# Moving the upper half of the attention weights from GpSimd to ScalarE

## The chip, the cores and the metric

One core of one Trainium2 chip runs the whole program. The metric is the device time of one launch in microseconds (us). The kernel before takes 861.48 us, the median of three runs (859.91 to 862.36).

## What is computed

Three layers in a row: an attention with a mask by hash buckets, a dense feed-forward with a gated activation, and a mixture of 8 experts of which each token takes two. Cut to what matters here:

```python
# attention: batch 2, heads 8, sequence 768, head size 64
mask = q_bucket[:, :, :, None] == k_bucket[:, :, None, :]
scores = np.where(mask, scale * q @ k.T, -1e9)
scores = scores - scores.max(-1, keepdims=True)
attn = np.exp(scores)
attn = attn / (attn.sum(-1, keepdims=True) + 1e-9)
x = attn @ v                       # becomes 1536 tokens of 512
# feed-forward, 512 -> 2048 -> 512
h = x @ w_in
x = (h / (1 + np.exp(-1.702 * h))) @ w_out
# experts: a noisy gate picks 2 of 8; 512 -> 1024 -> 512, relu between, weighted sum
```

## The kernel before

TensorE multiplies float16. To keep float32's accuracy, each factor is split into a high float16 part and a low one (the rest), and a product is three passes: high by high, high by low, low by high.

The attention runs in 96 units g = 0 to 95; a unit is one head and 128 queries, and 16 units make one chunk of 256 tokens. For a unit:

- `qk` (L252): TensorE makes the scores of 128 queries by 768 keys in PSUM (tile `s`, two buffers); the mask is part of the product.
- `rowmax` (L261, L262): VectorE takes the row's maximum and scales it (`mx`).
- `expo` (L271): ScalarE makes the exponentials into `e32` (two buffers), with the row's sum. From unit 28 on (`NG` = 28) VectorE makes the reciprocal of the sum from it at once (L275, L276); before, the sum is used later, behind the product.
- `e_hi` (L308), from unit 16 on: the **upper half**, `er[:, 0]`, float16, is `e32` times the reciprocal (or times 1.0 for units 16 to 27). GpSimd makes it. `er` has two buffers.
- `e_lo` (L319; L317 for units 16 to 27): the lower half, `er[:, 1]`, on VectorE (three of the units 16 to 27 on GpSimd). Behind it SyncE's queue issues a transposing DMA of both halves (L323) into `et`.
- `pv` (L364): TensorE multiplies the transposed weights by `v`.

So `e_hi` of unit g needs the exponential, the reciprocal, and that the transposing DMA of unit g-2 has read its buffer of `er`; and `expo` of unit g+2 needs that `e_lo` of unit g has read its buffer of `e32`.

The first 16 units take another way (float32, transposed on TensorE) and have no `e_hi`. Beside the attention run: the preparation of q and k (L142 to L209) and of v (L228 to L235), the splitting of the feed-forward's weights (L424 to L442), the feed-forward of the chunk before (L456 on TensorE, L474 on ScalarE, L486 on VectorE, L500 on ScalarE, L501 on GpSimd; then L467), and the routing (L586 to L679). After the attention come the last chunk's feed-forward, its routing, and the experts (L735 to L830), which TensorE fills.

Each engine works through its own queue in order. For the attention these orders aren't written out by hand: up to step 100 of the loop a planner orders each engine's instructions by the program's order and by its own estimate of when each one is ready. From step 100 on (the attention's last unit is 95) the order is that of the program.

`PARAM` holds the choices, among them the engine of `e_hi` by unit, `HI`, which is `'PPPP'[g%4]` in the line that counts (L56). `e_hi` itself has both ways already:

```python
        if PARAM["HI"](g) == "P":
            nc.gpsimd.tensor_scalar(er[:, 0], st[g]["e"], r, 1.0, op0=OP.mult, op1=OP.mult)
        else:
            nc.scalar.activation(er[:, 0], st[g]["e"], AF.Copy, scale=r)
```

Of the kernel before, what the change touches and what calls it, by code (L numbers as in the profile page):

```python
# [23 lines left out]
CAP = 432  # L24
REG = 256
# [29 lines left out]
PARAM = dict(GM=16, HE=lambda nm, b: 'D', OE=lambda nm, b: 'D', SC=lambda nm, b: 'D', WB=0, XO=lambda b: 'D', NG=16, WS=lambda i: 'P', TS=lambda g: True, XL=lambda g: 'D', GW=2, E0=7, T0=12, T1=16, EL=8, WX=3, PV={(1,2,3):4}, PVD=5, ST={}, VA={}, RA={}, O0=48, OS=2, IS=2, FU=16, VF=2, EC=lambda g: 'AA', QX=8, QS=3, EA=1, S1=(8,8,8,9,9,9,11,13), QE=8, XG=2, XB=2, PC=2, OH=3, BK=3, R0=18, R1=0, LK=8, WL=1, NW=3, LE=lambda nc: nc.scalar, I0=24, LQ=8, LV=0, W=[(g, 1) for g in range(-6, 30)], KA={(0,0,0):-8,(0,0,1):-6,(0,1,0):-4,(0,1,1):-2}, QA={(0,0,0):-7,(0,0,1):-3}, HI=lambda g: 'P', LO=lambda g: False)  # L55
PARAM.update(KA={(0, 0, 0): -15, (0, 0, 1): -6, (0, 1, 0): -5, (0, 1, 1): -4, (0, 2, 0): -1, (0, 2, 1): 1, (0, 3, 0): 4, (0, 3, 1): 5, (1, 0, 0): 37, (1, 0, 1): 39, (1, 1, 0): 44, (1, 1, 1): 46, (1, 2, 0): 42, (1, 2, 1): 51, (1, 3, 0): 47, (1, 3, 1): 51}, QA={(0, 0, 0): -15, (0, 0, 1): -3, (0, 0, 2): 1, (0, 0, 3): 3, (0, 1, 0): 8, (0, 1, 1): 9, (0, 1, 2): 17, (0, 1, 3): 21, (0, 2, 0): 24, (0, 2, 1): 28, (0, 2, 2): 30, (0, 2, 3): 33, (1, 0, 0): 37, (1, 0, 1): 41, (1, 0, 2): 47, (1, 0, 3): 52, (1, 1, 0): 57, (1, 1, 1): 56, (1, 1, 2): 60, (1, 1, 3): 69, (1, 2, 0): 72, (1, 2, 1): 69, (1, 2, 2): 80, (1, 2, 3): 84}, VA={(0, 0, 0): -1, (0, 0, 1): -3, (0, 1, 0): -1, (0, 1, 1): -1, (0, 2, 0): 0, (0, 2, 1): 0, (0, 3, 0): -1, (0, 3, 1): -2, (1, 0, 0): -1, (1, 0, 1): -1, (1, 1, 0): 2, (1, 1, 1): -4, (1, 2, 0): -3, (1, 2, 1): -3, (1, 3, 0): 2, (1, 3, 1): -2}, PV={(0, 0, 0): 4, (0, 0, 1): 5, (0, 0, 2): 6, (0, 0, 3): 5, (0, 1, 0): 6, (0, 1, 1): 4, (0, 1, 2): 4, (0, 1, 3): 5, (0, 2, 0): 5, (0, 2, 1): 5, (0, 2, 2): 5, (0, 2, 3): 6, (1, 0, 0): 4, (1, 0, 1): 5, (1, 0, 2): 4, (1, 0, 3): 5, (1, 1, 0): 5, (1, 1, 1): 5, (1, 1, 2): 5, (1, 1, 3): 6, (1, 2, 0): 6, (1, 2, 1): 4, (1, 2, 2): 4, (1, 2, 3): 4}, RA={0: 18, 1: 18, 2: 19, 3: 24, 4: 18}, W=[(g,1) for g in [-6, -4, -3, -1, 0, 0, 1, 1, 2, 4, 4, 7, 8, 8, 9, 10, 11, 12, 13, 14, 15, 16, 16, 17, 18, 20, 20, 22, 22, 23, 23, 24]], EC=lambda g:'AA', LE=lambda nc:nc.sync, HI=lambda g:'PPPP'[g%4], LO=lambda g:[0, 0, 0, 1, 0, 0, 0, 1][g%8]==1, S1=[8, 8, 8, 8, 8, 11, 13, 22], ST={0: 4, 1: 4, 2: 5, 3: 4, 4: 5, 5: 3}, NG=28, WS=lambda i:'PAAA'[i%4], HE=lambda nm,b:'DPDD'[2*(nm=='k')+b], OE=lambda nm,b:'DTDD'[2*(nm=='k')+b], SC=lambda nm,b:'DADD'[2*(nm=='k')+b], R1=2, I0=16, IS=2, O0=56, OS=1, GM=100, BK=3, OH=3, QX=8, QS=2, QE=7, VF=0, T0=12, T1=17, EL=10, WX=5, WL=2, PC=2, GW=2, E0=8, WB=2)  # L56


@with_exitstack
def fused(ctx: ExitStack, tc: tile.TileContext, q, k, v, proj, w_in, w_out, w_gate, w_noise, noise,  # L60
          w1, w2, out, dbg=None):
    nc = tc.nc
# [25 lines left out]
    def proj_parts():  # L88
        p32 = rt.tile([128, NBITS], F32, name="p32", tag="zc", bufs=1)
        nc.sync.dma_start(p32[:64], proj)  # L90
        nc.sync.dma_start(p32[64:], proj)
        # proj in three parts; the first ones of x and proj lie on grids, so that their products add exactly
        p3 = rt.tile([128, 3, NBITS], F16, name="p3", tag="z", bufs=1)
        nc.vector.tensor_scalar(p3[:, 0], p32, GP, GP, op0=OP.add, op1=OP.subtract)
        nc.vector.tensor_tensor(p32, p32, p3[:, 0], op=OP.subtract)
        nc.vector.tensor_copy(p3[:, 1], p32)
        nc.vector.tensor_tensor(p32, p32, p3[:, 1], op=OP.subtract)
        for nm, a0 in (("q", 0), ("k", 64)):
            w = pr[nm]
            h, l = slice(a0, a0 + 64), slice(64 - a0, 128 - a0)  # L100
            nc.vector.tensor_scalar(w[h, 0], p3[h, 0], SH, 0.0, op0=OP.mult, op1=OP.add)
            nc.vector.tensor_scalar(w[h, 1], p3[h, 1], -SH, 0.0, op0=OP.mult, op1=OP.add)
            nc.vector.tensor_scalar(w[h, 2], p32[h], -SH, 0.0, op0=OP.mult, op1=OP.add)
            nc.vector.memset(w[l, 0], 0.0)
            nc.vector.tensor_scalar(w[l, 1:3], p3[l, 0:2], -1.0 / SH, 0.0, op0=OP.mult, op1=OP.add)
# [3 lines left out]

# [1 line left out]
    raw, rows, kts, qts, vts, bks = {}, {}, {}, {}, {}, {}  # L111
    FL = "p h c d -> p (h c) d"

    # q: both heads of a pair, one chunk (u = pair, chunk); k and v: one head (u = pair, head)
    def load(nm, b, u):
# [12 lines left out]
    def stack_hi(nm, b, u):  # L128
        x = raw[nm, b, u]
        nh, n = (2, CT) if nm == "q" else (1, NT)  # L130
        if nm == "q":
            sa = att.tile([128, nh, n, 128], F16, name="qsa", bufs=1)
            sb = att.tile([128, nh, n, 128], F16, name="qsb", bufs=2)
        else:
            # in the place of what the feed-forward needs later, or no longer
            ks = moe.tile([128, 2, n, 128], F16, name="ks", tag="wraw" if b else "gt", bufs=PARAM["NW"] if b else 4)
            sa, sb = ks[:, 0:1], ks[:, 1:2]
# [75 lines left out]

    # the first units take float32 products, which need fewer passes of the other engines
    def v_load32(cc, hp):
# [20 lines left out]

# [1 line left out]
    st, ets, xts, pos, sms = {}, {}, {}, {}, {}  # L238
# [156 lines left out]

# [1 line left out]
    wi = [wts.tile([128, HP, FF], F16, name=f"wi{i}", tag="w") for i in range(2)]  # L397
# [105 lines left out]

# [1 line left out]
    before = consts.tile([128, 128], F16)  # L505
# [60 lines left out]
    def route(ci):  # L566
# [15 lines left out]
        zn = z[:, :, E:]  # L582
        # log(1 + exp(zn)) = max(zn, 0) + y with y = log(1 + t), t = exp(-|zn|), by Newton's steps
        w = rt.tile([128, 6, CT, E], F32, name="rw", bufs=1)
# [45 lines left out]
        yield  # L630
        # the row's last columns: token, first expert, both weights
        me = mst[ci, "xr"][:, :, 2 * DM:].bitcast(F32)
# [52 lines left out]

    # the first experts' first REG slots are read before the last chunk is routed: its tokens come behind them
    def reserve():
# [25 lines left out]

# [1 line left out]
    ew, eblk, xg, met, hts, yst = {}, {}, {}, {}, {}, {}  # L715
# [21 lines left out]

    # the slots of an expert: in one part, or in two
    def parts(e):
        return ((0, REG), (REG, CAP)) if e < EA else ((0, CAP),)  # L740

    def e_load(e, p):
# [12 lines left out]
        if nr:  # L755
            # the last 64 slots, twice; those that the tile before holds too go to spare rows
            nc.vector.tensor_copy(mf[:, nf], blank2)
            for h in range(2):
                nc.sync.dma_start(mf[h * 64 + 64 - nr:h * 64 + 64, nf], slots[r0 + 128 * nf:r0 + n, 2 * DM:])
# [73 lines left out]

# [1 line left out]
    todo, first, early = {}, {}, {}  # L835
# [22 lines left out]

    # the steps of several chains by turns
    def by_turns(chains):  # L860
# [49 lines left out]
    steps = {}  # L910
# [76 lines left out]
    for n, (e, p) in enumerate(gs):  # L987
        begin[e, p] = len(seq)
        c0, c1 = parts(e)[p]
        l1s = [("1", e, p, f) for f in range(FE // 128)]  # L990
        l2s = [("2", e, p, t) for t in range(c0 // 128, -(-c1 // 128))]
        # the next one's first product comes before this one's second
        if n and (p == 0 or n > EA):
            seq.insert(hold, l1s.pop(0))
        seq += l1s
        hold = len(seq)
        seq += l2s
# [33 lines left out]

# [1 line left out]
    most = nc.values_load(cnt_i[0:1, E:E + 1], min_val=0, max_val=N)  # L1033
    with tc.If(most > CAP):
        with tc.tile_pool(name="ov", bufs=1) as ov:
# [13 lines left out]
            with tc.For_i(0, E, 1) as e:  # L1049
# [5 lines left out]
                with tc.If(here > CAP):  # L1055
# [12 lines left out]
                    with tc.For_i(0, (OV + 127) // 128, 1) as k_:  # L1068
                        with tc.If(here > k_ * 128 + CAP):
                            # the row of this lane, or the last one of the expert  # L1070
                            nc.vector.tensor_tensor(val, blk, lane, op=OP.add)
# [10 lines left out]
                            me = row[:, 2 * DM:].bitcast(F32)  # L1082
                            # its token, or a spare row of the output
                            nc.vector.tensor_copy(tmp, me[:, 0:1].bitcast(I32))
                            nc.vector.scalar_tensor_tensor(tmp, tmp, float(N), lane, op0=OP.subtract, op1=OP.subtract)
                            nc.vector.tensor_tensor(tmp, tmp, ok, op=OP.mult)
                            nc.vector.scalar_tensor_tensor(ints[:, 1:2], tmp, float(N), lane, op0=OP.add, op1=OP.add)
                            # its weight
                            sc = 1.0 / (SX2 * SW1 * SW2)
# [51 lines left out]
```

## Time and profile before

| | |
|---|---|
| median of three runs | 861.48 us |
| profiled execution, first to last instruction | 857.1 us |
| TensorE busy | 734.4 us (86%) |
| VectorE busy | 563.0 us (66%) |
| ScalarE busy | 380.9 us (44%) |
| GpSimd busy | 358.5 us (42%) |
| units with an `e_hi` | 80, from 97.1 to 482.0 us |

The profile shows one execution. PE is TensorE's matrix products, PEld its weight loads, DVE VectorE, ACT ScalarE, POOL GpSimd, SP SyncE; a small q behind a name is the engine's sequencer. The chain of work that ended last is followed back from the last instruction, at each step to what released it. "Idle before" is how long an engine stood just before an instruction, and the name behind it is what ended that.

### The profile page before, as it was taken

To read this page: it belongs to the slowest core of one execution; us is meant where nothing else is said; L and a number is where in the kernel's file an instruction comes from. 1 tells how busy PE (TensorE), PEld (TensorE's weight loads), DVE (VectorE), ACT (ScalarE), POOL (GpSimd) and SP (SyncE) were. 2 spreads that over 40 slices of the span, in tenths; PEclk is the share of its full clock that TensorE was granted. 3 is DMA by queue.
4 is the path that set the end of the run, shared out by engine and by line. 5 is a ranking of instruction groups with operands and counts; after the bars stand their busy time and mean duration, and the time that the engine had idled before them with its cause. 6 is when DMAs were issued, how large, how long until landed. Compare 5 with 4: busy or idle time off the path is not lost.

```text
span 857.1 us, 14808 instructions
## 1 busy us (share of the span) xinstructions
PE 734.4 (86%) x5398; PEld 449.4 (52%) x5399; DVE 563.0 (66%) x1327; ACT 380.9 (44%) x779; POOL 358.5 (42%) x352
## 2 busy tenths in 40 slices
PE   1577687868888789888988999779999999999994
PEld 1354465436644565466567575546554555545542
DVE  8998799998997699579778626444533535335210
ACT  3687656545644464254335235243433534335210
POOL 6355478775846466456535333141021121211212
PEclk9878798999999989999999999989999999999997
DMA  8999999998989978986787533766875847757212
GB/s 202 224 246 234 208 212 209 220 196 157 182 150 200 170 150 184 234 159 112 131 150 118 106 141 112 185 184 158 222 158 171 205 110 202 160 163 167 37 13 39
DMA packets 285453, 141.03 MB, mean 165 GB/s; under 512 B 231552, under 2 KB 264384, under 8 KB 285376
## 3 DMA queue, kind: packets, MB, share of 16 engines
q1 hardware_dynamic: 278848, 126.37, 68.2%
q0 software_dynamic: 6528, 13.68, 8.7%
q8 instruction: 43, 0.70, 0.3%
q14 instruction: 34, 0.28, 0.1%
HBM read 61.49 MB, written 24.25 MB: 100 GB/s over the span
## 4 chain that ended last, share of the span: by engine, by line
PE 38%; DVE 29%; DMA 16%; issue 6%; POOL 5%; ACT 3%; SPq 1%; POOLq 0%; DVEq 0%; ACTq 0%
PE ph L792 16%; PE py L814 12%; DMA et<-er 6%; DVE er L319 6%; DVE mx L261 5%; PE h L456 4%; DMA slots<-xr,si 2%; PE py L818 2%; PE px L467 2%; POOL er L308 2%; POOL slots L679 2%; DMA qt<-qsb 2%; DMA out_dram<-yo,ti 2%; DVE wf L424 2%; ACT e L271 2%
## 5 line engine op out<-in xcount | busy, mean ns | idle before, releaser
L456 PE MATMUL h<-xt,wi 128*128 128x256 f16 x1152 | 145.6, 281 | 12.2 <-DVE th L486 8.2
L792 PE MATMUL ph<-xg,ew 128*128 128x432 f16 (+2 forms) x864 | 146.7, 334 | 9.5 <-DMA xg<-slots 9.5
L830 POOL DMA_INDIRECT out_dram<-yo,ti x32 | 52.7, 1648 | 231.3 <-ACT yo L828 168.8
L467 PE MATMUL px<-wo,gt 128*128 128x512 f16 x576 | 133.2, 382 | 5.9 <-ACT wo L441 3.3
L736 DVE SCALAR_TENSOR_TENSOR ew<-w,ew 128x1024 f16<-128x1024 f32 x64 | 77.9, 1226 | 89.3 <-ACT ew L735 89.3
L456 PEld LDWEIGHTS <-wi 128*128 128x128 f16 x1152 | 113.9, 101 | 36.4 <-issue 13.7
L271 ACT ACTIVATE e<-s,mx 128x768 f32<-128x768 f32 x96 | 86.0, 897 | 93.9 <-DVE mx L262 63.4
L814 PE MATMUL py<-ew,ht 128*128 128x512 f16 x576 | 125.8, 379 | 0.0
L792 PEld LDWEIGHTS <-ew 128*128 128x128 f16 x864 | 85.2, 101 | 69.1 <-issue 6.2
L252 PE MATMUL s<-kt,qt 128*128 128x512 f16 (+1 forms) x384 | 88.6, 354 | 26.6 <-ACT e L271 20.5
L308 POOL TENSOR_SCALAR er<-e,mx 128x768 f16<-128x768 f32 x68 | 69.1, 1017 | 88.7 <-DMA et<-er 29.5
L319 DVE SCALAR_TENSOR_TENSOR er<-e,mx,er 128x768 f16<-128x768 f32 x68 | 77.8, 1144 | 25.6 <-POOL er L308 25.5
L467 PEld LDWEIGHTS <-gt 128*128 128x128 f16 x576 | 55.3, 98 | 70.6 <-issue 9.2
L261 DVE TENSOR_REDUCE mx<-s 128x1 f32<-128x768 f32 x96 | 90.2, 944 | 2.1 <-PE s L252 2.0
L814 PEld LDWEIGHTS <-ht 128*128 128x128 f16 x576 | 56.4, 98 | 67.2
L803 DVE SCALAR_TENSOR_TENSOR ht<-ph,ht 128x432 f16<-128x432 f32 (+2 forms) x72 | 40.0, 556 | 57.0 <-ACT ht L802 56.1
L501 POOL TENSOR_TENSOR gt<-th,gt 128x512 f16<-128x512 f32 x48 | 61.0, 1270 | 34.2 <-ACT gt L500 33.2
L802 ACT ACTIVATE ht<-ph 128x432 f16<-128x432 f32 (+2 forms) x72 | 35.2, 490 | 84.3 <-PE ph L792 84.3
L735 ACT ACTIVATE ew<-w 128x1024 f16<-128x1024 f32 x64 | 66.3, 1047 | 2.5 <-DMA w<-in_moe_w_dram 2.5
L252 PEld LDWEIGHTS <-qt 128*128 128x128 f16 x384 | 37.2, 103 | 56.6 <-issue 31.1
L828 ACT ACTIVATE yo<-py,wv 128x512 f32<-128x512 f32 (+1 forms) x32 | 20.3, 633 | 102.7 <-PE py L814 54.6
L364 PE MATMUL pv<-et,vt 128*64 128x256 f16 x720 | 50.9, 280 | 8.7 <-DMA et<-er 7.3
(192 smaller groups left out, 958.1 us busy)
## 6 DMA issues: line engine op xcount, KB each, us to landing
w<-in_moe_w_dram SPq DMA_DIRECT2D x64, 512.0 KB, 4.2
wraw<-in_moe_w_in_dram SPq DMA_DIRECT2D x16, 512.0 KB, 4.3
wraw<-in_moe_w_out_dram SPq DMA_DIRECT2D x16, 512.0 KB, 5.1
slots<-zeros SPq DMA_DIRECT2D x27, 256.0 KB, 7.2
v<-in_v_dram SPq DMA_DIRECT2D x24, 192.0 KB, 4.1
out_dram<-zeros SPq DMA_DIRECT2D x13, 256.0 KB, 3.2
k<-in_k_dram SPq DMA_DIRECT2D x16, 192.0 KB, 3.0
q<-in_q_dram SPq DMA_DIRECT2D x48, 64.0 KB, 3.7
```

Source lines behind the costliest of these rows:

```text
L252: nc.tensor.matmul(ps[:, n0 * 128:n1 * 128], qt[:, s, h, t, :], kt[:, s, h, n0:n1, :].rearrange("p c t -> p (c t)"), start=(s == 0), stop= ...
L261: nc.vector.reduce_max(mx[:, 0:1], st[g]["ps"][:, :S], axis=AX.X)
L271: nc.scalar.activation(e32, st[g]["ps"][:, :S], AF.Exp, scale=0.125, bias=st[g]["mx"][:, 1:2], accum_out=sms[b, cc, hp][:, 2 * h + t:2 * h ...
L308: nc.gpsimd.tensor_scalar(er[:, 0], st[g]["e"], r, 1.0, op0=OP.mult, op1=OP.mult)
L319: nc.vector.scalar_tensor_tensor(er[:, 1], d["e"], d["mx"][:, 3:4], er[:, 0], op0=OP.mult, op1=OP.subtract)
L456: nc.tensor.matmul(ph[:, a, :], wi[ws][:, d, f0:f0 + 128], xt[:, d, xs, :], start=(d == 0 and ws == 0 and xs == 0), stop=(d == HP - 1 and ...
L467: nc.tensor.matmul(px, gts[ci, f // 2][:, gs, f % 2, t * 128:t * 128 + 128], wo[ws][:, f, :], start=(f == 0 and gs == 0 and ws == 0), stop ...
L501: nc.gpsimd.tensor_tensor(gt[:, 1], th, gt[:, 0], op=OP.subtract)
L735: nc.scalar.activation(hi, x, AF.Copy, scale=SW1 if j == 0 else SW2)
L736: nc.vector.scalar_tensor_tensor(lo, x, SW1 if j == 0 else SW2, hi, op0=OP.mult, op1=OP.subtract)
L792: nc.tensor.matmul(ph[:, :c1 - c0], w[:, ws, d * FE + f * 128:d * FE + f * 128 + 128], xg[e, p][:, xs * HP + d, :], start=(d == 0 and ws = ...
L814: nc.tensor.matmul(py, ht[:, f, hs, t * 128:t * 128 + 128], w[:, ws, f * DM:(f + 1) * DM], start=(i == 0), stop=(i == n - 1))
```

## The change

`HI` gives `A` for each unit: `e_hi` takes the other branch, an activation Copy with the reciprocal (or 1.0) as scale, in ScalarE's queue. All 80 of the GpSimd instructions at L308 become ScalarE instructions at L310. The rest of the diff removes comments. All other choices, buffers and orders in the program's text stay.

```diff
 PARAM.update(
...
-HI=lambda g:'PPPP'[g%4],
+HI=lambda g:'AAAA'[g%4],
...
 )
```

## Rows read from the trace of the kernel before

**Rows 1.** The page: busy time of each engine; the chain's shares by engine and line

```profile
PE 734.4 (86%) x5398; PEld 449.4 (52%) x5399; DVE 563.0 (66%) x1327; ACT 380.9 (44%) x779; POOL 358.5 (42%) x352
PE 38%; DVE 29%; DMA 16%; issue 6%; POOL 5%; ACT 3%; SPq 1%; POOLq 0%; DVEq 0%; ACTq 0%
PE ph L792 16%; PE py L814 12%; DMA et<-er 6%; DVE er L319 6%; DVE mx L261 5%; PE h L456 4%; DMA slots<-xr,si 2%; PE py L818 2%; PE px L467 2%; POOL er L308 2%; POOL slots L679 2%; DMA qt<-qsb 2%; DMA out_dram<-yo,ti 2%; DVE wf L424 2%; ACT e L271 2%
```

**Rows 2.** Windows: stretch, its length, busy time of each engine, clock, DMA share, GB/s

```profile
95.00:300.00 205.00, 166.00 (x1379) 107.14 (x1378) 182.27 (x402) 105.47 (x233) 131.27 (x117) 0.95 1.01 190
300.00:485.00 185.00, 165.69 (x1375) 110.53 (x1375) 149.91 (x403) 81.61 (x194) 100.44 (x93) 0.97 0.79 150
485.00:530.00 45.00, 44.63 (x345) 30.44 (x344) 16.05 (x56) 16.17 (x30) 13.25 (x13) 1.00 0.36 111
530.00:575.00 45.00, 35.27 (x219) 20.61 (x218) 23.29 (x78) 15.12 (x29) 14.50 (x17) 0.95 0.70 185
575.00:857.00 282.00, 269.48 (x1681) 147.09 (x1680) 106.55 (x190) 99.18 (x145) 50.03 (x31) 0.97 0.59 141
```

**Rows 3.** The chain that ended last, whole span, by line

```profile
by line: PE ph L792 16.1%; PE py L814 12.1%; DMA et<-er 6.4%; issue 6.3%; DVE er L319 5.7%; DVE mx L261 4.7%; PE h L456 3.5%; DMA slots<-xr,si 2.4%; PE py L818 2.2%; PE px L467 2.0%; POOL er L308 1.9%; POOL slots L679 1.9%; DMA qt<-qsb 1.8%
```

**Rows 4.** Groups by form: count, busy us, mean ns, idle before and its releasers

```profile
L308 POOL TENSOR_SCALAR er<-e,mx 128x768 f16<-128x768 f32 x68 | 69.1, 1017 | 88.7 <-DMA et<-er 29.5 <-DVE mx L276 19.0 <-DVE mx L275 6.0
L308 POOL TENSOR_SCALAR er<-e 128x768 f16<-128x768 f32 x12 | 12.4, 1029 | 6.6 <-DMA et<-er 5.2 <-PE pv L357 1.2
L319 DVE SCALAR_TENSOR_TENSOR er<-e,mx,er 128x768 f16<-128x768 f32 x68 | 77.8, 1144 | 25.6 <-POOL er L308 25.5
```

**Rows 5.** Timeline around 367 us: start us, us, engine, line; idle before

```profile
367.47 0.88 ACT L271 ACTIVATE e<-s,mx 128x768 f32<-128x768 f32 x1
...
368.35 0.89 ACT L271 ACTIVATE e<-s,mx 128x768 f32<-128x768 f32 x1
...
369.00 0.90 POOL L308 TENSOR_SCALAR er<-e,mx 128x768 f16<-128x768 f32 x1 [1.26 <-DVE mx L276]
...
369.22 0.59 ACT L474 ACTIVATE th<-h 128x512 f32<-128x512 f32 x1
```

**Rows 6.** Groups by form on ScalarE, whole span: copies of other widths, the exponential

```profile
L156 ACT ACTIVATE qsa<-q 128x256 f16<-128x256 f32 x24 | 9.9, 412 | 6.5 <-POOL q L143 4.4 <-issue 1.9
...
L735 ACT ACTIVATE ew<-w 128x1024 f16<-128x1024 f32 x64 | 66.3, 1047 | 2.5 <-DMA w<-in_moe_w_dram 2.5
...
L271 ACT ACTIVATE e<-s,mx 128x768 f32<-128x768 f32 x96 | 86.0, 897 | 93.9 <-DVE mx L262 63.4 <-DVE er L319 14.5 <-DVE mx L276 3.6
```

**Rows 7.** Three lines of VectorE: count, then ns min/median/max of one, first and last start

```profile
L319 DVE SCALAR_TENSOR_TENSOR er<-e,mx,er x68: 992/1018/2531, 172.0 to 483.2; 128x768 f16<-128x768 f32 x68
...
L198 DVE TENSOR_SCALAR qsb<-iota_i,bk x48: 216/232/1215, 238.7 to 454.0; 128x64 f16<-128x64 f16 x48
...
L424 DVE TENSOR_SCALAR wf<-wraw x32: 407/427/1377, 8.0 to 188.5; 128x512 int32<-128x512 int32 x32
```

**Rows 8.** Groups by form on VectorE, 95 to 485 us

```profile
L198 DVE TENSOR_SCALAR qsb<-iota_i,bk 128x64 f16<-128x64 f16 x48 | 15.0, 377 | 0.1
...
L424 DVE TENSOR_SCALAR wf<-wraw 128x512 int32<-128x512 int32 x15 | 11.2, 749 | 2.1 <-DMA wraw<-in_moe_w_out_dram 2.1
```

**Rows 9.** Windows of line L308 alone

```profile
95.00:485.00 390.00, 81.49 (x80) 0.96 0.91 171
```

**Rows 10.** Tile er: how long its transposing DMA takes to land, of 80

```profile
DMA to landing us min/median/max: 3.7/3.9/8.2
```

**Rows 11.** Timeline around 299 us

```profile
298.37 0.91 POOL L308 TENSOR_SCALAR er<-e,mx 128x768 f16<-128x768 f32 x1 [4.56 <-DMA et<-er]
...
299.31 1.02 DVE L319 SCALAR_TENSOR_TENSOR er<-e,mx,er 128x768 f16<-128x768 f32 x1 [3.73 <-POOL er L308]
299.80 1.30 POOL L308 TENSOR_SCALAR er<-e,mx 128x768 f16<-128x768 f32 x1 [0.52 <-DMA et<-er]
...
300.31 0.83 DVE L189 TENSOR_TENSOR pc<-pc,pow 128x36 f32<-128x36 f32 x1
...
300.51 0.90 ACT L271 ACTIVATE e<-s,mx 128x768 f32<-128x768 f32 x1 [5.75 <-DVE mx L262]
```

More of the change, by code (lines that the diff above doesn't have):

```diff
@@ L55 @@
 PARAM = dict(GM=16, HE=lambda nm, b: 'D', OE=lambda nm, b: 'D', SC=lambda nm, b: 'D', WB=0, XO=lambda b: 'D', NG=16, WS=lambda i: 'P', TS=lambda g: True, XL=lambda g: 'D', GW=2, E0=7, T0=12, T1=16, EL=8, WX=3, PV={(1,2,3):4}, PVD=5, ST={}, VA={}, RA={}, O0=48, OS=2, IS=2, FU=16, VF=2, EC=lambda g: 'AA', QX=8, QS=3, EA=1, S1=(8,8,8,9,9,9,11,13), QE=8, XG=2, XB=2, PC=2, OH=3, BK=3, R0=18, R1=0, LK=8, WL=1, NW=3, LE=lambda nc: nc.scalar, I0=24, LQ=8, LV=0, W=[(g, 1) for g in range(-6, 30)], KA={(0,0,0):-8,(0,0,1):-6,(0,1,0):-4,(0,1,1):-2}, QA={(0,0,0):-7,(0,0,1):-3}, HI=lambda g: 'P', LO=lambda g: False)
-PARAM.update(KA={(0, 0, 0): -15, (0, 0, 1): -6, (0, 1, 0): -5, (0, 1, 1): -4, (0, 2, 0): -1, (0, 2, 1): 1, (0, 3, 0): 4, (0, 3, 1): 5, (1, 0, 0): 37, (1, 0, 1): 39, (1, 1, 0): 44, (1, 1, 1): 46, (1, 2, 0): 42, (1, 2, 1): 51, (1, 3, 0): 47, (1, 3, 1): 51}, QA={(0, 0, 0): -15, (0, 0, 1): -3, (0, 0, 2): 1, (0, 0, 3): 3, (0, 1, 0): 8, (0, 1, 1): 9, (0, 1, 2): 17, (0, 1, 3): 21, (0, 2, 0): 24, (0, 2, 1): 28, (0, 2, 2): 30, (0, 2, 3): 33, (1, 0, 0): 37, (1, 0, 1): 41, (1, 0, 2): 47, (1, 0, 3): 52, (1, 1, 0): 57, (1, 1, 1): 56, (1, 1, 2): 60, (1, 1, 3): 69, (1, 2, 0): 72, (1, 2, 1): 69, (1, 2, 2): 80, (1, 2, 3): 84}, VA={(0, 0, 0): -1, (0, 0, 1): -3, (0, 1, 0): -1, (0, 1, 1): -1, (0, 2, 0): 0, (0, 2, 1): 0, (0, 3, 0): -1, (0, 3, 1): -2, (1, 0, 0): -1, (1, 0, 1): -1, (1, 1, 0): 2, (1, 1, 1): -4, (1, 2, 0): -3, (1, 2, 1): -3, (1, 3, 0): 2, (1, 3, 1): -2}, PV={(0, 0, 0): 4, (0, 0, 1): 5, (0, 0, 2): 6, (0, 0, 3): 5, (0, 1, 0): 6, (0, 1, 1): 4, (0, 1, 2): 4, (0, 1, 3): 5, (0, 2, 0): 5, (0, 2, 1): 5, (0, 2, 2): 5, (0, 2, 3): 6, (1, 0, 0): 4, (1, 0, 1): 5, (1, 0, 2): 4, (1, 0, 3): 5, (1, 1, 0): 5, (1, 1, 1): 5, (1, 1, 2): 5, (1, 1, 3): 6, (1, 2, 0): 6, (1, 2, 1): 4, (1, 2, 2): 4, (1, 2, 3): 4}, RA={0: 18, 1: 18, 2: 19, 3: 24, 4: 18}, W=[(g,1) for g in [-6, -4, -3, -1, 0, 0, 1, 1, 2, 4, 4, 7, 8, 8, 9, 10, 11, 12, 13, 14, 15, 16, 16, 17, 18, 20, 20, 22, 22, 23, 23, 24]], EC=lambda g:'AA', LE=lambda nc:nc.sync, HI=lambda g:'PPPP'[g%4], LO=lambda g:[0, 0, 0, 1, 0, 0, 0, 1][g%8]==1, S1=[8, 8, 8, 8, 8, 11, 13, 22], ST={0: 4, 1: 4, 2: 5, 3: 4, 4: 5, 5: 3}, NG=28, WS=lambda i:'PAAA'[i%4], HE=lambda nm,b:'DPDD'[2*(nm=='k')+b], OE=lambda nm,b:'DTDD'[2*(nm=='k')+b], SC=lambda nm,b:'DADD'[2*(nm=='k')+b], R1=2, I0=16, IS=2, O0=56, OS=1, GM=100, BK=3, OH=3, QX=8, QS=2, QE=7, VF=0, T0=12, T1=17, EL=10, WX=5, WL=2, PC=2, GW=2, E0=8, WB=2)
@@ new lines @@
+PARAM.update(KA={(0, 0, 0): -15, (0, 0, 1): -6, (0, 1, 0): -5, (0, 1, 1): -4, (0, 2, 0): -1, (0, 2, 1): 1, (0, 3, 0): 4, (0, 3, 1): 5, (1, 0, 0): 37, (1, 0, 1): 39, (1, 1, 0): 44, (1, 1, 1): 46, (1, 2, 0): 42, (1, 2, 1): 51, (1, 3, 0): 47, (1, 3, 1): 51}, QA={(0, 0, 0): -15, (0, 0, 1): -3, (0, 0, 2): 1, (0, 0, 3): 3, (0, 1, 0): 8, (0, 1, 1): 9, (0, 1, 2): 17, (0, 1, 3): 21, (0, 2, 0): 24, (0, 2, 1): 28, (0, 2, 2): 30, (0, 2, 3): 33, (1, 0, 0): 37, (1, 0, 1): 41, (1, 0, 2): 47, (1, 0, 3): 52, (1, 1, 0): 57, (1, 1, 1): 56, (1, 1, 2): 60, (1, 1, 3): 69, (1, 2, 0): 72, (1, 2, 1): 69, (1, 2, 2): 80, (1, 2, 3): 84}, VA={(0, 0, 0): -1, (0, 0, 1): -3, (0, 1, 0): -1, (0, 1, 1): -1, (0, 2, 0): 0, (0, 2, 1): 0, (0, 3, 0): -1, (0, 3, 1): -2, (1, 0, 0): -1, (1, 0, 1): -1, (1, 1, 0): 2, (1, 1, 1): -4, (1, 2, 0): -3, (1, 2, 1): -3, (1, 3, 0): 2, (1, 3, 1): -2}, PV={(0, 0, 0): 4, (0, 0, 1): 5, (0, 0, 2): 6, (0, 0, 3): 5, (0, 1, 0): 6, (0, 1, 1): 4, (0, 1, 2): 4, (0, 1, 3): 5, (0, 2, 0): 5, (0, 2, 1): 5, (0, 2, 2): 5, (0, 2, 3): 6, (1, 0, 0): 4, (1, 0, 1): 5, (1, 0, 2): 4, (1, 0, 3): 5, (1, 1, 0): 5, (1, 1, 1): 5, (1, 1, 2): 5, (1, 1, 3): 6, (1, 2, 0): 6, (1, 2, 1): 4, (1, 2, 2): 4, (1, 2, 3): 4}, RA={0: 18, 1: 18, 2: 19, 3: 24, 4: 18}, W=[(g,1) for g in [-6, -4, -3, -1, 0, 0, 1, 1, 2, 4, 4, 7, 8, 8, 9, 10, 11, 12, 13, 14, 15, 16, 16, 17, 18, 20, 20, 22, 22, 23, 23, 24]], EC=lambda g:'AA', LE=lambda nc:nc.sync, HI=lambda g:'AAAA'[g%4], LO=lambda g:[0, 0, 0, 1, 0, 0, 0, 1][g%8]==1, S1=[8, 8, 8, 8, 8, 11, 13, 22], ST={0: 4, 1: 4, 2: 5, 3: 4, 4: 5, 5: 3}, NG=28, WS=lambda i:'PAAA'[i%4], HE=lambda nm,b:'DPDD'[2*(nm=='k')+b], OE=lambda nm,b:'DTDD'[2*(nm=='k')+b], SC=lambda nm,b:'DADD'[2*(nm=='k')+b], R1=2, I0=16, IS=2, O0=56, OS=1, GM=100, BK=3, OH=3, QX=8, QS=2, QE=7, VF=0, T0=12, T1=17, EL=10, WX=5, WL=2, PC=2, GW=2, E0=8, WB=2)
```

## The prediction

> **What bounds the kernel now.** I read the page first. TensorE is busy for 86% of the span, yet of the chain that ended last it holds only 38%, VectorE 29% and DMA 16% [rows 1]; so the bound differs by stage. The windows by stage show how: from 575 us on TensorE is busy for 269.48 of 282.00 us, in 485 to 530 for 44.63 of 45.00; in the attention, 95 to 300, VectorE is busy for 182.27 of 205.00, and in 300 to 485 both are high, TensorE 165.69 and VectorE 149.91 of 185.00 [rows 2]. All 80 instructions at L308 lie in 95 to 485 [rows 9]. What this change is worth is read there; what is gained or lost there moves the later stages, which TensorE fills, by the same amount.
>
> In that stretch no engine is full all the time; the units are held by a ring. The chain by line names its links: the transposing DMA of `er` 6.4%, the lower half L319 5.7%, the maximum L261 4.7%, and the upper half L308 1.9% [rows 3]. The timeline around 299 us shows one turn: GpSimd stood 4.56 us until a DMA had freed `er`, the lower half on VectorE stood 3.73 us for the upper one, and the next exponential on ScalarE 5.75 us for VectorE [rows 11]; there all engines stand for one transfer. Over the run GpSimd stood 88.7 + 6.6 = 95.3 us before L308, 29.5 + 5.2 of it for that DMA, much of the rest for the reciprocal; VectorE stood 25.6 us before L319, nearly all of it for L308 [rows 4].
>
> **What is removed.** GpSimd loses 81.5 us [rows 9]. It is no bound: its lines hold 5% of the chain, L308 1.9% of that [rows 1, 3]. Two gains follow.
>
> First, VectorE is slowed by GpSimd. An operation that takes a median of 1.018 us (L319), 0.232 (L198) or 0.427 (L424) has instances of 2.531, 1.215 and 1.377 [rows 7]; at 300.31 us a small product takes 0.83 us while L308 runs for 1.30 instead of 0.9 [rows 11]. The means above the medians give 68 x 0.126 = 8.6 us for L319 [rows 4, 7], 48 x 0.145 = 7.0 for L198 and 15 x 0.322 = 4.8 for L424 [rows 7, 8], together 20.4 us. L308 is 81.5 of GpSimd's 231.7 busy us in the stretch [rows 2, 9], 35%, and I put 35% of the stretching on it: 7.2 us. The bounds are 0 and all 20.4. How much of VectorE's time reaches the end: its part of the chain is 29% of 857.1 = 249 us, and it is busy for 563.0 - 23.3 - 106.6 = 433 us before 530 [rows 1, 2], so 57%. Gain 4.1 us, at most 11.6.
>
> Second, the upper half itself gets shorter. ScalarE's copies in SBUF take 412 ns for 256 columns and 1047 for 1024 [rows 6], 0.827 ns for each further column, so 768 columns take 412 + 423 = 835 ns; the exponential of the same width, which reads a column of its own per row too, takes 897 and is the upper bound. 80 x 0.835 = 66.8 us against 81.5, 14.7 less. L308 is on the chain for 1.9% of 857.1 = 16.3 us of its 81.5, 20%: gain 2.9 us. Both gains together: 7.0 us, at most 14.5.
>
> **What is added.** ScalarE gets 66.8 us in one in-order queue. It is busy for 105.5 + 81.6 = 187.1 of 390 us in the stretch [rows 2], so there is room, but not at each moment. 48% of 66.8 us, 32.0 us, fall on time in which ScalarE has other work, and either the upper half or that work is late by so much. The timeline at 367 us shows such a place: two exponentials back to back, the upper half at 369.00 while the second runs until 369.24, then the feed-forward's tanh [rows 5]. What a late upper half costs I take from the lower half, which stood 25.5 us for the 81.5 of L308 [rows 4, 9], 31%: 32.0 x 0.31 = 9.9 us. The bounds are 20%, L308's own part of the chain (6.4 us), and VectorE's 57% (18.2).
>
> The waits move too. The 95.3 us that GpSimd stood at the head of its queue [rows 4] are now stood in ScalarE's. Behind the waiting instruction are the next exponential, the tanh L474 and the copy L500 of the feed-forward, and L481; waiting for these are the reciprocal, VectorE's L486 and through it TensorE's next L456. Where VectorE stood as well (25.5 us) nothing is lost more. Of the other 69.8 us, 48% meet a ScalarE that had work, 33.5 us, and of that I take the exponential's part of the chain: 2% of 857.1 = 17.1 of its 86.0 us [rows 1, 6], 20%: 6.7 us. It can be 0, where the planner puts the waiting copy behind all that is ready, and 95.3 x 0.48 x 0.57 = 26 us at most.
>
> At nothing I cost: the DMA itself, which SyncE issues behind the lower half as before and which lands in 3.9 us, up to 8.2 [rows 10]; GpSimd's other work and its row scatters, which come no later than before; and the stages before 95 and behind 485 us, which have no L308. If the lower half came late by a whole wait, the DMA would be issued later behind other transfers in SyncE's queue; that is in the upper bound.
>
> **The sum.** 9.9 + 6.7 - 7.0 = +9.6 us. The span goes from 857.1 to 866.7; the median of the runs stands 4.4 us above the profiled span, so 871 us. By the bounds: 6.4 + 0 - 14.5 = -8 us, 853, and 18.2 + 26 - 7.0 = +37 us, 899.
>
> **The rivals.**
>
> *Faster.* ScalarE's idle 203 us take the copies in and VectorE is freed. It decides where the planner finds the copy a place at which ScalarE stands anyway, as at 299 us, where it stood 5.75 us [rows 11]. For it: VectorE is the fuller engine until 300 us. Against it: the waits before L308. Both losses go to nothing and the gain is 7.0 to 14.5 us; middle, 861.5 - 10.7 = 851 us. The page "SBUF — State Buffer" of the Trainium skill, section "SBUF: two separate sides", gives this rival its rule: VectorE and GpSimd share one pair of ports as an exclusive lock, and ScalarE's own ports never wait on anyone. The stretched rows agree that the two block each other; by the rule alone there is a gain and nothing against it. But the rule speaks of ports, and the terms above that decide the sign are of queues.
>
> *No change.* The ring by the DMA sets the pace: upper half 0.9, lower half 1.0 and landing 3.9 us make 5.8 us, up to 10.1 with the slowest landing [rows 5, 7, 10], for two units, which take 2 x 390 / 80 = 9.8 us now. Then who makes the upper half doesn't matter: 861 us.
>
> *Much slower.* The planner's order on ScalarE is the upper half of a unit ahead of the next exponential. At 368.35 us that exponential would wait until the upper half ends at 369.90, 1.55 us [rows 5]. It decides if half of the 80 units have it: 40 x 1.55 = 62 us, of which 31% = 19 us reach the end, on top of the forecast: 890 us. For it: the text of the program has the upper half right behind its exponential. Against it: the planner holds an instruction back until it deems it ready.
>
> **How the numbers follow.** Chances: the forecast 0.38 (its own range 864.1 to 880), faster 0.28, no change 0.18, much slower 0.16. About 0.3% of the time, 2.6 us, is what a measurement can tell from no change. So faster 0.28, same 0.18, slower 0.38 + 0.16 = 0.54. The range reaches into both outer cases, 849 to 890, and leaves out about 0.09 at each end. All of it hangs on an order of instructions that no trace of before shows; this is why it is wide for a sum of a few microseconds.
>
> **What would show it.** In the profile after: 80 copies at L310 on ScalarE of 0.83 to 0.90 us, no L308; L319's mean down from 1.144 us by about 0.04 to 0.12; ScalarE idle before L310 for tens of microseconds, on `er`'s DMA and on the reciprocal; VectorE idle before L319 on L310 for more than 25.6 us; and the exponential, L474 and L500 later behind it. The last unit's lower half would end near 494 us instead of 484 [rows 7]. I am wrong if ScalarE's waits before L310 are short and VectorE's total falls by more than 10 us while its idle time doesn't grow; then the lock was the larger term.

## The result, and the profile after

The kernel after takes 852.05 us, the median of four runs (851.51 to 853.96); the kernel before, run beside it, 861.34. The medians lie 9.3 us apart; the ratio is 0.990, and its 95% interval, 0.988 to 0.992, is a gain of 6.6 to 10.2 us. I had forecast 871 and slower; the time lies where the rival *Faster* put it, 851.

The page of the kernel after, busy time and share of each engine; before's line is in [rows 1]:

```profile
span 849.4 us, 14814 instructions
...
PE 734.0 (86%) x5398; PEld 447.3 (53%) x5399; DVE 541.0 (64%) x1327; ACT 443.5 (52%) x859; POOL 270.9 (32%) x272
```

GpSimd lost 87.6 us, ScalarE gained 62.6 (the copies take 73.3, in part overlapped with their neighbours), and VectorE, to whose queue nothing was added and from which nothing was taken (1327 instructions as before), lost 22.0 us of busy time. That last number is what the experiments follow.

The windows by stage of the kernel after (stretch, its length, busy time of each engine, clock, DMA share, GB/s), against [rows 2]:

```profile
95.00:300.00 205.00, 169.01 (x1412) 109.03 (x1413) 171.25 (x406) 136.73 (x278) 87.51 (x77) 0.93 1.00 193
300.00:485.00 185.00, 170.98 (x1395) 111.03 (x1394) 139.74 (x400) 112.31 (x230) 55.51 (x52) 0.97 0.80 150
```

VectorE is busy for 11.0 us less in the first stretch and 10.2 less in the second, 171.25 for 182.27 and 139.74 for 149.91, and TensorE gets more done, 169.01 for 166.00 and 170.98 for 165.69. The attention ends earlier by as much as the whole kernel. The lower halves of units 28 to 95 in the kernel after (ns min/median/max of one, first and last start):

```profile
L319 DVE SCALAR_TENSOR_TENSOR er<-e,mx,er x68: 992/1018/1786, 171.8 to 475.6; 128x768 f16<-128x768 f32 x68
```

The first starts where it did before (172.0 us), the last at 475.6 instead of 483.2 [rows 7], and the span is shorter by 7.7 us. So the gain arises in these units.

The groups by form of the kernel after (count, busy us, mean ns, idle before and its releasers), against [rows 4, 6]:

```profile
L271 ACT ACTIVATE e<-s,mx 128x768 f32<-128x768 f32 x96 | 85.7, 894 | 34.0 <-DVE mx L262 19.7 <-DVE xr L653 5.0 <-DVE er L317 4.4
...
L319 DVE SCALAR_TENSOR_TENSOR er<-e,mx,er 128x768 f16<-128x768 f32 x68 | 71.2, 1049 | 24.3 <-ACT er L310 22.6 <-issue 0.9
...
L310 ACT ACTIVATE er<-e,mx 128x768 f16<-128x768 f32 x68 | 63.3, 934 | 38.1 <-DMA et<-er 24.2 <-DVE mx L276 8.0 <-DVE top L614 2.1
...
L198 DVE TENSOR_SCALAR qsb<-iota_i,bk 128x64 f16<-128x64 f16 x48 | 12.2, 320 | 0.1
...
L310 ACT ACTIVATE er<-e 128x768 f16<-128x768 f32 x12 | 10.0, 837 | 3.6 <-DMA et<-er 3.6
```

Three things are to be read here. The lower half's mean fell from 1144 to 1049 ns, near its median of 1018: VectorE is hardly held up in it any more. ScalarE now stands 38.1 + 3.6 = 41.7 us before the upper half, but before the exponential only 34.0 us where it stood 93.9 [rows 6]: its waits together didn't grow, 75.7 us for 93.9; they stand at another place of the queue. And the lower half's own wait is the same, 24.3 us for 25.6, now for ScalarE.

### The profile page after: what moved, and what is told of

The parts are those of the page before. It is cut to its first block, busy times and chain, and to the rows that moved or that the text cites. A ratio compares the mean times of both kernels' runs of the same rounds, so it can differ in the third digit from the quotient of the medians.

```text
span 849.4 us, 14814 instructions
## 1 busy us (share of the span) xinstructions
PE 734.0 (86%) x5398; PEld 447.3 (53%) x5399; DVE 541.0 (64%) x1327; ACT 443.5 (52%) x859; POOL 270.9 (32%) x272
## 5 line engine op out<-in xcount | busy, mean ns | idle before, releaser
L456 PE MATMUL h<-xt,wi 128*128 128x256 f16 x1152 | 139.8, 276 | 2.0 <-DVE th L486 1.7
L467 PE MATMUL px<-wo,gt 128*128 128x512 f16 x576 | 134.9, 388 | 7.2 <-ACT wo L441 3.9
L456 PEld LDWEIGHTS <-wi 128*128 128x128 f16 x1152 | 112.1, 99 | 24.8 <-issue 5.5
L252 PE MATMUL s<-kt,qt 128*128 128x512 f16 (+1 forms) x384 | 90.6, 362 | 18.6 <-ACT e L271 14.6
L319 DVE SCALAR_TENSOR_TENSOR er<-e,mx,er 128x768 f16<-128x768 f32 x68 | 71.2, 1049 | 24.3 <-ACT er L310 22.6
L310 ACT ACTIVATE er<-e,mx 128x768 f16<-128x768 f32 x68 | 63.3, 934 | 38.1 <-DMA et<-er 24.2
L364 PE MATMUL pv<-et,vt 128*64 128x256 f16 x720 | 53.8, 283 | 13.9 <-DMA et<-er 13.9
```

The costliest lines, as they stand in the source:

```text
L252: nc.tensor.matmul(ps[:, n0 * 128:n1 * 128], qt[:, s, h, t, :], kt[:, s, h, n0:n1, :].rearrange("p c t -> p (c t)"), start=(s == 0), stop= ...
L319: nc.vector.scalar_tensor_tensor(er[:, 1], d["e"], d["mx"][:, 3:4], er[:, 0], op0=OP.mult, op1=OP.subtract)
L364: nc.tensor.matmul(po[h * 64:h * 64 + 64, 0, :], vt[:, c, vs, h * 64:h * 64 + 64], et[h][:, es * NT + c].rearrange("p t q -> p (t q)"), st ...
L456: nc.tensor.matmul(ph[:, a, :], wi[ws][:, d, f0:f0 + 128], xt[:, d, xs, :], start=(d == 0 and ws == 0 and xs == 0), stop=(d == HP - 1 and ...
L467: nc.tensor.matmul(px, gts[ci, f // 2][:, gs, f % 2, t * 128:t * 128 + 128], wo[ws][:, f, :], start=(f == 0 and gs == 0 and ws == 0), stop ...
```

## The experiments

Two theories stood against each other and against a third. *Lock*: GpSimd's operation slows VectorE while both run, and that is what the change took away. *Queue*: the upper half, or what stands behind it on GpSimd, came late in GpSimd's queue. *Order*: the planner orders everything anew when one engine's work changes, and this time it was lucky. Times are medians. A ratio, and a difference in us unless another is named, is against the kernel before as it ran beside that experiment, since that kernel's own median lay between 861.34 and 862.68 us. By this the kernel after gains 9.3 us. A page or timeline is of one execution, whose time can lie some microseconds from the median.

**Is it the order? e6 and e7.** In both, the two steps of the loop that put the upper half and the steps called soon are swapped in the program's text, in e6 of the kernel before, in e7 of the kernel after.

```diff
-            e_hi(g + 1)
         for f, a in first.pop(g, []):
             f(*a)
+        if 0 <= g + 1 < NU:
+            e_hi(g + 1)
```

> The kernel before with the upper half's instruction put a few lines later in the program's text (behind the steps that the loop calls soon); no instruction is added, removed or moved to another engine, only the planner's order can differ. Lock and queue theory: 861, within 3 us. Order theory: it moves by more than 4 us, to either side.

> The kernel after with the same lines swapped as in the run before it. Lock and queue theory: 852, within 3 us, and 9 us below the run e6. Order theory: the gap to e6 isn't 9 us; it can have either sign.

e6 took 862.86 us, ratio 0.999 (0.997 to 1.002); e7 855.47, ratio 0.992 (0.989 to 0.995). Neither moved beyond its interval from the kernel that it was built on, and the gap between them is 7.4 us; e7's median lies 0.5 us outside the 3 us that were allowed. These two new orders are worth no 9 us; the order theory falls as the main cause. An order is not worth nothing: e7's five runs spread from 851.93 to 859.54.

**Each load by itself, first try: e4 and e5.** e4 is the kernel after with GpSimd's old copy added, e5 the kernel before with ScalarE's copy added; nobody reads what they write. Each leaves the output as it is.

```diff
+        if g >= NG:
+            xx = moe.tile([128, 512], F32, name="wf", bufs=1).bitcast(F16)[:, :S]
+            nc.gpsimd.tensor_scalar(xx, st[g]["e"], r, 1.0, op0=OP.mult, op1=OP.mult)   # e4
+            nc.scalar.activation(xx, st[g]["e"], AF.Copy, scale=r)                      # e5
```

> The kernel after, plus GpSimd's old copy in units 28 to 95 (68 times), written to a scratch tile that nothing reads: GpSimd works beside VectorE again, but nobody waits for its result. If the gain of the change is the freed VectorE (lock theory): VectorE's busy time goes from 541 back to about 560 us, L319's mean from 1049 to about 1140 ns, and the time from 852 to about 859. If the gain is that the upper half no longer stands in GpSimd's queue (queue theory): VectorE is stretched as well, yet the time stays within 3 us of 852. If it is a luckier order of the planner (order theory): no size is forecast, 843 to 862.

> The kernel before, plus ScalarE's copy of the same size in units 28 to 95 (68 times), written to a scratch tile that nothing reads; the true upper half stays on GpSimd. It prices ScalarE's load alone. By the prediction's two loss terms (9.9 + 6.7 us for 80 copies): 68/80 of them, 14 us more than before, 875. If ScalarE has room for the copies: 861, within 3 us. By the order theory: 852 to 871.

e4 took 867.47 us, ratio 1.005 (1.003 to 1.006): the whole gain and 5 us more are gone, though the upper half is on ScalarE. VectorE's busy time came back as the lock theory had it, 561.9 us, with a mean of 1116 ns for the lower half; but the time lies 8 us above that theory's 859, and further from the queue theory's 852. e5 took 868.01, ratio 1.006 (1.004 to 1.007), 5.3 us more than before and far from the 14 of the loss terms. Its page:

```profile
PE 738.6 (85%) x5398; PEld 450.1 (52%) x5399; DVE 560.1 (65%) x1327; ACT 438.8 (51%) x847; POOL 357.5 (41%) x352
```

Both are not clean: the added copy reads the exponential, so it holds that buffer, and its scratch space is that of the weights' unpacking, for which the first copies have to wait (e4's first starts at 191.8 us). So the same was done again without either.

**Each load by itself, clean: e8 and e9.** 60 operations of the same size in units 36 to 95 read a constant tile instead (128 columns, six times); the reciprocal as scale ties them to their unit.

```diff
+        if g >= 36:
+            xx = moe.tile([128, 512], F32, name="wf", bufs=1).bitcast(F16)[:, :S] ...
+            xi = ident32[:, None, :].to_broadcast([128, NT, 128])
+            nc.gpsimd.tensor_scalar(xx, xi, r, 1.0, op0=OP.mult, op1=OP.mult)   # e8, on after
+            nc.scalar.activation(xx, xi, AF.Copy, scale=r)                      # e9, on before
```

> The kernel after, plus 60 GpSimd operations of the old size (units 36 to 95) that read a constant tile and write a scratch tile nothing reads; only their scale ties them to the unit's reciprocal. Against e4 they no longer hold the exponential's buffer, and they start when the feed-forward's weights are done with the scratch space. Lock theory (GpSimd's mere work beside VectorE costs): VectorE's busy time in 95 to 485 us up by about 9 to 12 us over after, time 859 to 863. If e4's loss came from the held buffer or the scratch space instead: 852, within 3 us.

> The kernel before, plus the same 60 operations on ScalarE (a copy of a constant tile into scratch, with the unit's reciprocal as scale): ScalarE's load alone, without the held buffer of e5. By the prediction's loss terms: 60/80 of 16.6 = 12 us more, 874. By e5's +5 us for 68: 4 us, 866. If e5's loss was the held buffer: 862, within 3 us.

e8 took 861.05 us, ratio 0.998 (0.997 to 1.000), 1.3 us below before: 60 operations that nobody waits for give back 8.0 us of the 9.3. Its page, the engines' line:

```profile
PE 736.9 (86%) x5398; PEld 449.3 (52%) x5399; DVE 560.3 (65%) x1327; ACT 445.7 (52%) x859; POOL 334.1 (39%) x332
```

VectorE is back at 560.3 us, 19.3 more than in the kernel after, with the same 1327 instructions; from 95 to 485 us it is busy for 325.0, 14.0 more, where 9 to 12 were expected. e9 took 868.26 us, ratio 1.007 (1.005 to 1.010): 60 copies on ScalarE cost 6.0 us, 0.10 us each. Its page:

```profile
PE 737.2 (85%) x5398; PEld 448.9 (52%) x5399; DVE 569.2 (66%) x1327; ACT 431.0 (50%) x839; POOL 359.0 (41%) x352
```

So there is a price for ScalarE's load, as forecast, but half of the 12 us. VectorE is busy for longer too, 569.2 for 563.0; but in e5, which loses nearly as much, it is busy for less, 560.1, so VectorE's time can't be all of the price. What the rest is, no run shows.

**Lock or queue: e12.** e8 leaves open whether VectorE is slowed, or GpSimd's other work comes late behind the added operations. e12 keeps GpSimd as busy, with a fill that reads no tile.

```diff
+        if g >= 36:
+            xx = moe.tile([128, 512], F32, name="wf", bufs=1).bitcast(F16)
+            nc.gpsimd.tensor_scalar(xx[:, 0:1], r, 1.0, 1.0, op0=OP.mult, op1=OP.mult)
+            nc.gpsimd.memset(xx, 0.0)
```

> The kernel after, plus in units 36 to 95 a GpSimd fill of 1024 float16 columns of the scratch tile (estimated at 0.9 us from the fills of 128 and 256 columns in the trace of before), behind a one-column operation that ties it to the reciprocal. As long as e8's operation, but it reads no tile. Lock theory, if reading is what collides: VectorE isn't stretched, 852 to 855. Queue theory (GpSimd's other work comes late): as e8, 861. If writing collides as well: VectorE is stretched as in e8, 861.

It took 852.24 us, ratio 0.989 (0.987 to 0.991): nothing is lost. Its page, the engines' line:

```profile
PE 732.8 (86%) x5398; PEld 446.9 (53%) x5399; DVE 540.9 (64%) x1327; ACT 443.9 (52%) x859; POOL 348.7 (41%) x392
```

The added fills in the groups by form of the same kernel:

```profile
L314 POOL MEMSET wf<- 128x1024 f16 x60 | 57.1, 951 | 3.1
```

GpSimd is busy for 348.7 us, more than in e8 (334.1), and VectorE for 540.9, as in the kernel after (541.0). The part of the queue theory that speaks of what stands behind the upper half would have lost time here; it falls. The other part, that the upper half itself came late, the traces answer: from the end of the reciprocal to the start of the upper half, units 28 to 95 together took 114.6 us before and 116.5 after. On ScalarE it starts no sooner. The two timelines show the difference between copy and fill (start us, us). In e8 a lower half that starts while GpSimd's copy runs takes 1.41 us:

```profile
379.20 0.91 POOL L314 TENSOR_SCALAR wf<-ident,mx 128x768 f16<-128x768 f32 x1 [0.19 <-DVE mx L276]
379.50 1.41 DVE L323 SCALAR_TENSOR_TENSOR er<-e,mx,er 128x768 f16<-128x768 f32 x1 [0.48 <-ACT er L310]
```

In e12 one that starts while the fill runs takes 1.02, its median; but four of L198, which have a single wide input, start during a fill and all end behind it, within 0.1 us (here L323 is the lower half, as the added lines move it down):

```profile
354.43 0.95 POOL L314 MEMSET wf<- 128x1024 f16 x1
354.64 0.83 DVE L198 TENSOR_SCALAR qsb<-iota_i,bk 128x64 f16<-128x64 f16 x4
...
361.36 0.95 POOL L314 MEMSET wf<- 128x1024 f16 x1
361.67 1.02 DVE L323 SCALAR_TENSOR_TENSOR er<-e,mx,er 128x768 f16<-128x768 f32 x1 [0.72 <-ACT er L310]
```

The same four by themselves (ns min/median/max of one; alone it takes about 230):

```profile
L198 DVE TENSOR_SCALAR qsb<-iota_i,bk x4: 391/576/770, 354.6 to 355.1; 128x64 f16<-128x64 f16 x4
```

All of VectorE's instructions can be counted in this way. Take for each its time behind the end of the one before it, and compare it with the median of those of its line and form that ran with no GpSimd instruction beside them; call it lengthened when it takes over 0.1 us more. With no GpSimd instruction beside, none is lengthened in any run (of 675 before, 835 after).

| VectorE instructions that start while ... runs | lengthened | by, us |
|---|---|---|
| before: L308 | 36 of 131 | 21.0 |
| before: another of GpSimd's | 110 of 372 | 68.5 |
| after: any of GpSimd's | 107 of 377 | 64.5 |
| e8: an added copy | 29 of 93 | 14.6 |
| e12: an added fill | 5 of 97 | 3.1 |

VectorE's 22.0 us are thus nearly all the 21.0 that stood beside L308. In e12 the few that a fill lengthens have a single wide input; none is a lower half, of which 20 start during a fill. So it is not GpSimd's being busy that costs most, but its reading beside VectorE. The page "SBUF — State Buffer" of the Trainium skill, section "Who interferes with whom", says that a VectorE operation with two inputs in SBUF collides with a GpSimd operation that reads SBUF and not with one that only writes; this trace agrees, 1.41 us against 1.02.

**Which half collides: e1 and e11.** e1 puts every other unit's upper half on ScalarE, the odd ones; e11 the even ones.

```diff
-HI=lambda g:'AAAA'[g%4],
+HI=lambda g:'PAPA'[g%4],    # e1: odd units on ScalarE
+HI=lambda g:'APAP'[g%4],    # e11: even units on ScalarE
```

> Every other unit's upper half on ScalarE, the others on GpSimd. Lock theory with a small price for ScalarE's load: half of the gain, 857, within 3 us. Order theory: anything from 848 to 868.

> The other half: ScalarE makes the even units' upper halves, GpSimd the odd ones'. In the trace of before 14 of the 40 odd units have an upper half that is stretched over 1.05 us, and 6 of the 40 even ones: the odd one runs while VectorE makes the even one's lower half. Lock theory: the half that keeps the odd ones on GpSimd keeps most collisions, 857 to 861, at least 3 us above e1. If any half does as well as the other (ScalarE's and GpSimd's load alone): 853 to 856.

e1 took 853.60 us, ratio 0.989 (0.986 to 0.991), e11 856.68, ratio 0.994 (0.993 to 0.996). Against the kernel before that is 8.7 and 5.3 us: half of the copies moved gives nearly the whole gain in e1, 0.4 us more than the lock theory allowed, and 57% of it in e11, at 0.3 us below the range given. The difference between them, 0.6% with intervals apart, has the sign that the lock theory gave it, by which the odd unit's upper half runs beside the even one's lower half. A pair in the kernel before, on the timeline:

```profile
354.19 1.00 DVE L319 SCALAR_TENSOR_TENSOR er<-e,mx,er 128x768 f16<-128x768 f32 x1
354.43 1.53 POOL L308 TENSOR_SCALAR er<-e,mx 128x768 f16<-128x768 f32 x1 [4.87 <-DVE mx L276]
356.00 1.02 DVE L319 SCALAR_TENSOR_TENSOR er<-e,mx,er 128x768 f16<-128x768 f32 x1 [0.81 <-POOL er L308]
```

GpSimd's upper half takes 1.53 us instead of 0.9, since VectorE has begun first, and the next lower half stands 0.81 us for it. Of what GpSimd keeps, 34 of L308 take a mean of 974 ns in e1 and 1038 in e11:

```profile
L308 POOL TENSOR_SCALAR er<-e,mx 128x768 f16<-128x768 f32 x34 | 33.1, 974 | 69.9 <-DVE mx L276 27.3 <-DMA et<-er 26.3 <-DVE pc L189 5.9
```

```profile
L308 POOL TENSOR_SCALAR er<-e,mx 128x768 f16<-128x768 f32 x34 | 35.3, 1038 | 81.4 <-DMA et<-er 37.4 <-DVE mx L276 18.5 <-ACT er L310 9.2
```

VectorE bears out little of the difference. Beside L308 its instructions are lengthened by 7.3 us in e1 and 9.4 in e11, its busy time is 551.1 and 553.2, and the lower half is even the longer one in e1, a mean of 1158 ns for 1128, since there it meets other work of GpSimd. The executions profiled took 856.17 and 854.88 us, so these rows don't hold the 3 us. That e1 reaches the full gain isn't explained by ScalarE's smaller load either (414.5 us for 443.5 after), since e11 has it as well, 412.4. It stays open.

**A faster one? e10, e13, e14.** If GpSimd's reading is what costs, more of it might go.

```diff
-HE=lambda nm,b:'DPDD'[2*(nm=='k')+b],
+HE=lambda nm,b:'DDDD'[2*(nm=='k')+b],    # e10, e13, e14: rounding of q, second batch, on VectorE
-WS=lambda i:'PAAA'[i%4],
+WS=lambda i:'AAAA'[i%4],                 # e10 alone: scaling of the weights on ScalarE
```

> The kernel after with two more groups taken off GpSimd: the rounding of q of the second batch (12 at L142, 1.1 us each) goes to VectorE (0.47 us each as its twelve there take before), and the scaling of 8 weight blocks (L438, 0.85 us) to ScalarE. Lock theory: VectorE gains 5.6 us of work but loses stretching; the chain of before holds L142 in 300 to 485 us; 848 to 853. If only the upper half mattered: 852, within 3 us, or slower by VectorE's 5 us.

> The kernel after, with only the rounding of q of the second batch moved from GpSimd (12 at L142) to VectorE; the weights' scaling stays on GpSimd, unlike e10. Lock theory: 13.5 us less of GpSimd against 5.6 us more of VectorE, 849 to 853. If e10's loss was this move and not the weights: 857 to 860.

> e1 (odd units on ScalarE) and e13's move together, a candidate for the fastest. Lock theory: e1's time less what e13 gains over after, 850 to 854. Otherwise no better than e1, 854 or more.

e13 took 854.52 us, ratio 0.991 (0.990 to 0.993): 1.5 us above what the lock theory gave and no better than the kernel after. Its VectorE is busy for 548.0 us, 7.0 more than after: the rounding's own 5.6 us were not bought back. e10 took 859.06, ratio 0.998 (0.996 to 0.999), outside all that was expected: it gains 3.3 us, e13 7.5, so eight scalings of 0.67 us more on ScalarE cost 4.2. e14, e13's move on e1, took 856.71, ratio 0.994 (0.992 to 0.996). None beats the kernel after; e1 equals it.

The pages of e10 and e14, and e10's lower halves (first and last start at the end):

```profile
PE 730.1 (85%) x5398; PEld 446.3 (52%) x5399; DVE 542.8 (63%) x1339; ACT 447.9 (52%) x867; POOL 251.8 (29%) x252
```

```profile
PE 735.2 (86%) x5398; PEld 448.8 (53%) x5399; DVE 561.8 (66%) x1339; ACT 413.6 (49%) x819; POOL 301.6 (35%) x300
```

```profile
L319 DVE SCALAR_TENSOR_TENSOR er<-e,mx,er x68: 991/1017/1544, 187.9 to 483.3; 128x768 f16<-128x768 f32 x68
```

They show that VectorE's busy time alone doesn't set the time. e14's VectorE is as busy as e8's (561.8 and 560.3 us), yet e14 gains 5.3 us and e8 1.3. e10's is as free as after's, and from the first of these lower halves to the last it takes 295.4 us, for 303.8 after and 311.2 before; but the first starts 16 us later than after. Its loss lies ahead of these units.

## Why the prediction was wrong

**What bounds the kernel** held. The gain arose in the attention and came through the rest one for one (lower half 7.6 us earlier, span 7.7 us shorter).

**First gain, VectorE freed: the size failed.** The step took the 20.4 us of three groups for all the stretching there was, and put 35% of it on L308: 7.2 us. VectorE's busy time fell by 22.0 us, more than the bound. By the count above the stretching beside GpSimd was some 90 us, 21.0 of them beside L308. In the three groups L308's part is near the forecast: 0.7 us of L319, 5.1 of L198 and 1.9 of L424, 7.7 in all. The other 13.3 us lie in 18 further lines, none over 1.8 us, which I had not summed. L319's own mean fell from 1144 to 1049 ns mostly because it met GpSimd's other work less often, and for this I had no term.

The way from busy time to the end came out somewhat lower than the 57% that I took. e8 against after gives 8.0 us of time for 19.3 us of VectorE, 41%; with that, 22.0 us are worth 9.1. It is no constant, as e10 and e14 show.

**Second gain, a shorter copy: small and overestimated.** With a constant scale the copy takes 837 ns, as worked out from the neighbouring widths; with the reciprocal as scale, in 68 of 80, it takes 934, over my upper bound of 897. The 80 take 73.3 us instead of 66.8, 8.2 less than GpSimd's; by the step's 20% that is 1.6 us for 2.9.

**What is added: the loss terms failed.** 9.9 us for copies that meet a busy ScalarE and 6.7 for waits moved into its queue, 16.6 for 80. e9 measured the load alone: 6.0 us for 60, so 8.0 for 80, and e5 5.3 for 68, 6.2 for 80. e9 holds waits as well, 11.7 us before its added copies, 10.5 of it for the reciprocal, but not those for `er`'s DMA. The waits as a whole didn't do what the step said: I counted 48% of 69.8 us as lost because ScalarE had other work. But ScalarE stood 93.9 us before its exponentials already, in the kernel before, for the same ring. After, it stands 34.0 there and 41.7 before the upper half, 75.7 in all, less than before. As I read it, a wait that an engine would have had one instruction later costs nothing when it is had here; no run takes the waits by themselves. VectorE's idle time before L319, which I said would grow, is 24.3 us for 25.6.

The sum with the measured sizes, -9.1 - 1.6 + 6.2 to 8.0, gives -4.5 to -2.7 us, against -9.3. The sign comes out; some 5 to 7 us stay open. e8 and e9 show the same gap: they carry nearly the same copies (80 on ScalarE and 60 on GpSimd, 60 and 80), by the prices so far less than 1 us apart, and lie 7.2 us apart. So about 6 us may hang on which engine makes the upper half that the lower half waits for, though the unclean pair, e4 and e5, lies only 0.5 us apart. A candidate is that the lock holds up GpSimd too (ns min/median/max of one, before and after):

```profile
L308 POOL TENSOR_SCALAR er<-e,mx x68: 896/905/1672, 170.3 to 482.0; 128x768 f16<-128x768 f32 x68
```

```profile
L310 ACT ACTIVATE er<-e,mx x68: 918/935/957, 169.6 to 474.7; 128x768 f16<-128x768 f32 x68
```

GpSimd's upper half takes up to 1.67 us, ScalarE's never over 0.96. No run tests this by itself.

**The rivals.** *Faster* was right in time, 851, and in its reason: the rule on the shared ports, which I set aside because it "speaks of ports" while the sign hung on queues, named the larger term. It was given 0.28 by a sum in which that term was 4.1 instead of about 9 us. That its 851 us is nearly the measured time is in part luck: it set both losses to nothing, and e9 measured 6.0 us for 60 copies. *No change*, the DMA ring, was refuted: the waits for that DMA stay (29.5 + 5.2 us before, 24.2 + 3.6 after), yet the units got faster, so the ring doesn't set the pace in all of them. *Much slower*: its condition came, its price didn't. In the kernel after, 39 of 79 upper halves start ahead of the next unit's exponential, the half that it asked for, yet ScalarE stands less before the exponentials than before.

**What I named as proof that I was wrong** came in two of three points: VectorE's total fell by more than 10 us and its idle time before L319 didn't grow. ScalarE's waits before the upper half, 41.7 us, weren't short.

## What to carry to other kernels

Where an engine that holds the chain runs the same operations for longer than their medians, look for a neighbour that reads the same memory beside it, and price a move by the stretch, in all lines, of those instructions that start while the neighbour's runs (here 21.0 us, for 22.0 measured), not by a few large groups. In this kernel a GpSimd copy that reads SBUF cost time even when nobody waits for its result (e8: 8.0 us for 60), while a fill cost the kernel none (e12). Before waits that move into another engine's queue are counted, look whether that engine stands for the same cause already.

## What the runs showed of the hardware

ScalarE's copy of 768 float32 columns to float16 takes 837 ns with a constant scale and 934 with a scale per row. I had not expected the 97 ns; the page "ScalarE: Activation LUTs" of the Trainium skill, section "What ACT_TABLE_LOAD costs", gives about 93 ns for each such operand, and the traces agree.

GpSimd's fill of 1024 float16 columns takes 951 ns. None of VectorE's 20 lower halves that start during one in e12 is lengthened, while 9 of 15 that start during e8's copy of 768 float32 columns are, by 3.9 us in all. Some instructions with a single wide input are held until the fill ends: four of L198 took 391 to 770 ns instead of about 230.
